# Masks behind both heads' products, inverse sums a step later, and a reordered turn to the routed mixture

## The chip, the cores and the metric

The kernel runs on one core of a Trainium2 chip. The metric is device time in microseconds (us), the median of several runs. The profile is one execution on the same kind of core. Its engines are called PE (TensorE matmuls), PEld (TensorE weight loads), DVE (VectorE), ACT (ScalarE), POOL (GpSimd) and SP (SyncE, which here only issues DMAs). Each engine takes its instructions in the order in which they were written, and stands when the next one has to wait.

## The reference, cut to what matters

Three layers follow one another on 1152 tokens of 512 numbers.

```python
# 1. attention, 2 batches x 8 heads, 576 positions, 64 wide, with a decay
scores = scale * q @ k.T
decay  = cum[:, None] - cum[None, :]              # cum: running sum of log f
scores = where(causal, -1e9, scores + decay)
attn   = exp(scores - max(scores)); attn /= attn.sum(-1) + 1e-9
x      = attn @ v
# 2. dense mixture, 4 experts of 512 -> 1024 -> 512, every token through all of them
out   += p[:, e] * (relu(x @ w1[e]) @ w2[e])
# 3. routed mixture, 8 experts: tokens with x @ w_skip <= 0 pass through,
#    the others go through the one expert with the largest logit
y[mask] = gate_w[mask] * (relu(xc[mask] @ w1[e]) @ w2[e]);  out = x + y
```

## The kernel before, in words

**Attention** (span 0 to about 115 us) goes over eight pairs of heads, numbered 0 to 7, and in each over five steps. Steps 0 to 3 take 128 queries each against 128, 256, 384 and 512 keys, head by head; step 4 takes the last 64 queries of both heads together. `emit_s` (line 238) writes a step's scores: for each head a product with the rounded keys (L247, tile kh), a product with what the rounding left over (L248, kl), and a bf16 product that adds the causal mask (L249); the three add into one PSUM tile. Then DVE adds the bias and finds the maximum (L252, tile sn), and ACT takes the exponential and its sum (L255, tile e). Step 4 does the same with L266 to L278 and the tile e_t. At the end of step 4, DVE adds 1e-9 to the sums of the whole pair (L281, rs) and inverts them (L282), and ACT spreads them into a tile rsx (L284).

`emit_tp` (line 287) follows two steps behind: PE transposes the exponentials (L298; for step 4 L309 and L313), ACT copies the first head's result out of PSUM (L301, tile et) and DVE the second head's (L303). With step 4 PE also transposes rsx (L321) and the inverse sums (L322). `emit_av` (line 332) follows three steps behind with the products with v. The loop at line 470 writes, for each step n, first `emit_tp` of step n-2, then `emit_s` of step n, then `emit_av` of step n-3, and then what prepares the next pair.

That preparation is `split_k` and `split_q` (lines 215 and 226): DVE rounds the next pair's keys (L224, kh) and queries (L229, qa), and POOL subtracts the rounded from the full values (two of L232 into kl, two of L235 into qa, 64 partitions each). For pair 1 they are written in step 2 of pair 0, for the others in step 0 of the pair ahead. From pair 4 on, steps 1 and 4 also split a quarter of a weight tile of the dense mixture: an ACT cast (L146) and a POOL subtraction (L150).

**The dense mixture** (about 115 to 525 us) runs up products (L660 to L662) and down products (L675 to L677) back to back on PE. Nothing of it is edited.

**The turn** (about 525 to 538 us) finds each token's expert for the last blocks of tokens. `select` (L766) collects the first expert's tokens on PE, `logits` (L557) and `prefix` (L585, L587) are small PE products, `choose`, `keep`, `mine` and `pick` small DVE steps, and `heat` (L731) writes matmuls whose result nothing reads. Meanwhile the weights of the routed mixture arrive: SP loads them in chunks of 1 MB (L136) into a ring of 18 places.

**The routed mixture** (about 533 us to the end) goes over eight small tiles (`Few`, one for each expert, up to 64 tokens) and two larger ones for the rest (`Many`). For a tile, POOL gathers its tokens (L503), PE turns them (`x_in`, L879, copied out of PSUM by ACT in L880), `up` (L886) multiplies with the first weights in two halves, `turn` (L893) transposes, and `down` (L901) multiplies with the second weights. `place`, `spread` and `lists` (L994 to L1022) find which tokens the larger tiles take. From the second tile on, POOL also fetches weights of the larger tiles (L861), by an index that is only known then.

Of the kernel before, what the change touches and what calls it, by code (L numbers as in the profile page):

```python
# [13 lines left out]
ALU = mybir.AluOpType  # L14
# [32 lines left out]
def kernel(  # L47
# [116 lines left out]
    with ExitStack() as at:  # L164
# [61 lines left out]
        def split_q(p):  # L226
            raw, qa, kh, kl = [state[p][x] for x in ("raw", "qa", "kh", "kl")]
            rk = raw[:, QW:QKW].rearrange("p (h c) -> p h c", h=2)
            V.tensor_copy(out=qa, in_=raw[:, 0:QW])  # L229
            for h in range(2):  # L230
                rows = slice(64 * h, 64 * h + 64)
                G.tensor_tensor(out=kl[rows, h], in0=rk[rows, h], in1=kh[rows, h].bitcast(F32), op=ALU.subtract)  # L232
            for h in range(2):
                rows, cols = slice(64 - 64 * h, 128 - 64 * h), slice(TOPAD * h, TOPAD * h + TOPAD)
                G.tensor_tensor(out=qa[rows, cols], in0=raw[rows, cols], in1=qa[rows, cols].bitcast(F32),  # L235
                                op=ALU.subtract)

        def emit_s(p, i):
            st = state[p]
            qa, kh, kl, bi = st["qa"], st["kh"], st["kl"], st["bi"]  # L240
            if i < 4:
                w = P * (i + 1)
                n = max(256, w)
                for h in range(2):
                    ps = ps_s.tile([P, 512], F32, tag="s", name=f"s_{p}_{i}_{h}")
                    q0 = TOPAD * h + i * P
                    T.matmul(out=ps[:, :n], lhsT=qa[:, q0:q0 + P], rhs=kh[:, h, :n], start=True, stop=False)  # L247
                    T.matmul(out=ps[:, :n], lhsT=qa[:, q0:q0 + P], rhs=kl[:, h, :n], start=False, stop=False)  # L248
                    T.matmul(out=ps[:, i * P:w], lhsT=identb, rhs=maskd, start=False, stop=True)  # L249
                    sneg = e_p.tile([P, S], F32, tag="sneg", name=f"sn_{p}_{i}_{h}")  # L250
                    mn = sm_p.tile([P, 1], F32, tag="mn", name=f"mn_{p}_{i}_{h}")
                    V.tensor_tensor_reduce(out=sneg[:, :w], in0=ps[:, :w], in1=bi[:, h, :w], scale=-0.125,  # L252
                                           scalar=3.0e38, op0=ALU.add, op1=ALU.min, accum_out=mn)
                    e = e_p.tile([P, S], F32, tag=f"e{h}", name=f"e_{p}_{i}_{h}")
                    A.activation(out=e[:, :w], in_=sneg[:, :w], func=AF.Exp, bias=mn, scale=-1.0,  # L255
                                 accum_out=st["sum"][:, 2 * i + h:2 * i + h + 1])
                    st["E"][i, h] = e
            else:
                sneg = e_p.tile([P, S], F32, tag="sneg", name=f"sn_{p}_t")
                mns = []  # L260
                for half in range(2):
                    c0 = half * 288
                    ps = ps_s.tile([P, 512], F32, tag="s", name=f"s_{p}_t_{half}")
                    for h in range(2):
                        q0 = TOPAD * h + 512
                        T.matmul(out=ps[:, :288], lhsT=qa[:, q0:q0 + P], rhs=kh[:, h, c0:c0 + 288], start=(h == 0),  # L266
                                 stop=False)
                        T.matmul(out=ps[:, :288], lhsT=qa[:, q0:q0 + P], rhs=kl[:, h, c0:c0 + 288], start=False,
                                 stop=(half == 0 and h == 1))
                    if half == 1:  # L270
                        T.matmul(out=ps[:, 224:288], lhsT=identb, rhs=maskt, start=False, stop=True)
                    mn = sm_p.tile([P, 1], F32, tag="mn", name=f"mn_{p}_t_{half}")
                    V.tensor_tensor_reduce(out=sneg[:, c0:c0 + 288], in0=ps[:, :288], in1=bi[:, 2, c0:c0 + 288],
                                           scale=-0.125, scalar=(3.0e38 if half == 0 else mns[0]),
                                           op0=ALU.add, op1=ALU.min, accum_out=mn)
                    mns.append(mn)
                e = e_p.tile([P, S], F32, tag="e0", name=f"e_{p}_t")
                A.activation(out=e, in_=sneg, func=AF.Exp, bias=mns[1], scale=-1.0,  # L278
                             accum_out=st["sum"][:, 8:9])
                st["E"][4] = e  # L280
                V.tensor_scalar(out=st["rs"], in0=st["sum"], scalar1=1e-9, scalar2=None, op0=ALU.add)  # L281
                V.reciprocal(out=st["sum"], in_=st["rs"])  # L282
                rsx = st["rs"] = sm_p.tile([P, 4, P], F32, tag="rsx", name=f"rsx_{p}", bufs=1)
                A.copy(out=rsx.rearrange("p j (h c) -> p (j h) c", h=2),  # L284
                       in_=st["sum"][:, 0:8].unsqueeze(2).to_broadcast([P, 8, 64]))

        def emit_tp(p, i):
            st = state[p]
# [181 lines left out]
        for n in range(2, len(steps) + LAG_AV):  # L470
            if 0 <= n - LAG_TP < len(steps):
                emit_tp(*steps[n - LAG_TP])
            if n < len(steps):
                p, i = steps[n]
                emit_s(p, i)
# [50 lines left out]
    with ExitStack() as mo:  # L526
# [237 lines left out]
        def select(t):  # L764
            for g in range(2):
                T.matmul(out=xsel[RT * g:RT * g + RT, 0:HD], lhsT=sel[:, t - NX, :],  # L766
                         rhs=acc[:, t, g * HD:(g + 1) * HD], start=(t == NX), stop=(t == L))
# [4 lines left out]
        choose(L - 1)  # L772
        mine(L - 1)
        count(L - 1)
        for t in range(NX, NA):
            select(t)
        logits(L, ps_u.tile([P, 512], F32, tag="u", name=f"lg_{L}"))
        keep(L - 1)
        prefix(L - 1, pf)
        heat(6)  # L780
        choose(L)
        pf = ps_u.tile([P, 512], F32, tag="u", name="pf_L")
        prefix(L, pf)
        mine(L)
        pick(L - 1)
        select(L - 1)
        pick(L)
        select(L)
# [20 lines left out]
    xes = [xs0] + [xe_p.tile([P, HD], F32, name=f"xe_{e}") for e in range(1, E2)]  # L809
    xos = [xe_p.tile([P, DM], F32, name=f"xo_{k}") for k in range(KO)]  # L810
    G.memset(xes[1], 0.0)
    for x in xes[2:]:
        A.copy(out=x, in_=zero.to_broadcast([P, HD]))
    xt_p = pool(ctx, "xt", 1, "right")
    wraw2 = pool(ctx, "wraw2", 4, "right")
    for k in range(14, RING):
# [199 lines left out]
        V.tensor_tensor(out=gt, in0=f[:, :, 4], in1=gt, op=ALU.add)  # L1016

    def lists():
        po = tpx[:, 0:KO * 5 * E2].rearrange("p (k j e) -> p k j e", k=KO, j=5)
        for t in range(NB):  # L1020
            for k in range(KO):
                T.matmul(out=po[:, k], lhsT=oho[:, t, k, :], rhs=perm[:, t, :, :], start=(t == 0 and k == 0),  # L1022
                         stop=(t == NB - 1 and k == KO - 1))
        listed(po, KO, idxo, gato)
# [4 lines left out]
    load_m(14, NS + 2)  # L1029
    tiles[0].up(0)  # L1030
    tiles[0].up(1)
    for x in xos:
        A.copy(out=x, in_=zero.to_broadcast([P, DM]))
    gates()
    tiles[0].turn()
    tiles[1].x_in()
    tiles[0].down()
    place()
    tiles[1].up(0)
    tiles[1].up(1)  # L1040
    spread(0, NB)
    tiles[2].x_in()
    ahead = {E2 - 3: (0, 0), E2 - 2: (1, 0), E2 - 1: (0, 1), E2: (1, 1)}
    behind = [i for i in range(len(chunks)) if chunks[i][1] >= E2]
    for i in range(1, len(tiles)):
# [115 lines left out]
```

## Time and profile before

| | |
|---|---|
| median of 3 runs | 633.64 us (633.6 to 636.07) |
| the profiled execution's own time | 633.03 us |
| its span | 631.3 us |
| mean granted TensorE clock | 0.991 |
| PE busy | 613.6 us (97%) |
| DVE busy | 251.1 us (40%) |
| ACT busy | 202.1 us (32%) |
| POOL busy | 177.6 us (28%) |

The profile's times are those of one execution, in us from the start of the span. A row of the timeline gives start, duration, engine, line, operation, output and inputs, shapes, and how many instructions of one kind were merged into it (x8). A bracket tells how long the engine had been idle before and what ended that. PE's ends are modelled: matmuls overlap, so what a matmul costs is the distance from its start to the next one's. PEclk is the granted clock as a share of 2.4 GHz: 1.00 is the upper of the two levels, 0.50 the lower (1.2 GHz).

### The profile page before, as it was taken

The page shows a single profiled execution, that of the slowest core. Times are in us where ns is not written, and L with a number is a line of the kernel's source. Part 1 is how long each engine was busy: PE and PEld are TensorE (multiplying, and loading weights), DVE is VectorE, ACT ScalarE, POOL GpSimd, SP SyncE. Part 2 cuts the span into 40 slices and gives each one's busy share as a digit, 9 for nine tenths or more (in the row PEclk, how much of TensorE's full clock was granted, in tenths as well). Part 3 has the DMA queues.
Part 4 walks back from the last instruction along what each step waited for, and adds up shares of the span by engine and source line. Part 5 has one row for each costly group of instructions (what it writes and reads, how often), then busy time and mean ns, then how long its engine had stood idle before and what let it go on. Part 6 is the DMA issues. An engine that isn't in the chain of part 4 may idle for free. (4 is left out here: it accounts for less than half of the span.)

```text
span 631.3 us, 9528 instructions
## 1 busy us (share of the span) xinstructions
PE 613.6 (97%) x3773; PEld 514.6 (82%) x3773; DVE 251.1 (40%) x686; ACT 202.1 (32%) x480; POOL 177.6 (28%) x160
## 2 busy tenths in 40 slices
PE   8899999999999999999999999999999999899995
PEld 5788777988899999999999999998888975455674
DVE  6777776222222222222222222222223577411753
ACT  5678887422122122122122122112202112211661
POOL 5755883223033033033023013102200000532411
PEclk7999999999999999999999999999999999999998
DMA  6768570211011021001201101205705457999930
GB/s 205 225 249 307 194 245 2 69 66 67 0 67 68 0 67 41 26 7 61 67 1 66 67 1 66 67 0 226 308 17 214 169 188 268 360 422 423 413 144 24
DMA packets 20415, 86.50 MB, mean 137 GB/s; under 512 B 3086, under 2 KB 4120, under 8 KB 13200
## 3 DMA queue, kind: packets, MB, share of 16 engines
q1 hardware_dynamic: 14816, 69.52, 29.8%
q0 software_dynamic: 2240, 10.32, 4.1%
q10 hardware_dynamic: 3312, 6.03, 2.6%
q8 instruction: 30, 0.49, 0.3%
q14 instruction: 17, 0.14, 0.1%
HBM read 79.44 MB, written 7.64 MB: 138 GB/s over the span
## 5 line engine op out<-in xcount | busy, mean ns | idle before, releaser
L150 POOL TENSOR_TENSOR wl<-raw,wh 128x512 fp32r<-128x512 f32 x64 | 82.8, 1294 | 272.4 <-ACT wh L146 272.4
L663 ACT ACTIVATE hh<-u 128x384 fp32r<-128x384 f32 x96 | 47.2, 491 | 298.9 <-PE u L662 294.9
L661 PE MATMUL u<-xtl,wh 128*128 128x384 f32 x384 | 129.4, 337 | 0.0
L662 PE MATMUL u<-xth,wl 128*128 128x384 f32 x384 | 129.2, 337 | 0.0
L660 PE MATMUL u<-xth,wh 128*128 128x384 f32 x384 | 129.2, 336 | 0.0
L675 PE MATMUL dn<-wh,hh 128*128 128x512 f32 x288 | 114.8, 399 | 0.0
L676 PE MATMUL dn<-wl,hh 128*128 128x512 f32 x288 | 113.8, 395 | 0.0
L677 PE MATMUL dn<-wh,hl 128*128 128x512 f32 x288 | 113.3, 393 | 0.0
L664 DVE SCALAR_TENSOR_TENSOR hl<-u,hh 128x384 fp32r<-128x384 f32 x96 | 53.5, 557 | 149.6 <-ACT hh L663 149.5
L687 DVE SCALAR_TENSOR_TENSOR acc<-dn,dps,acc 128x512 f32<-128x512 f32 (+1 forms) x64 | 47.4, 742 | 109.9 <-PE dn L677 109.9
L661 PEld LDWEIGHTS u<-xtl,wh 128*128 128x128 f32 x384 | 72.2, 188 | 1.0
L660 PEld LDWEIGHTS u<-xth,wh 128*128 128x128 f32 x384 | 72.2, 188 | 0.9
L662 PEld LDWEIGHTS u<-xth,wl 128*128 128x128 f32 x384 | 72.2, 188 | 0.0
L677 PEld LDWEIGHTS dn<-wh,hl 128*128 128x128 f32 x288 | 54.1, 188 | 12.3
L675 PEld LDWEIGHTS dn<-wh,hh 128*128 128x128 f32 x288 | 54.1, 188 | 10.8
L676 PEld LDWEIGHTS dn<-wl,hh 128*128 128x128 f32 x288 | 54.2, 188 | 10.2
L255 ACT ACTIVATE e<-sn,mn 128x128 f32<-128x128 f32 (+3 forms) x64 | 35.6, 557 | 14.8 <-DVE mn L252 14.6
L146 ACT CAST wh<-raw 128x512 fp32r<-128x512 f32 x64 | 39.2, 612 | 0.0
L252 DVE CUSTOM_DVE_ANT_0 sn<-s,bias 128x128 f32<-128x128 f32 (+3 forms) x64 | 29.3, 485 | 7.6 <-PE s L249 4.8
L886 PE MATMUL up<-wm,xt 128*64 128x512 f32 x128 | 30.3, 598 | 0.9 <-ACT xt L880 0.6
L901 PE MATMUL yp<-wm,ht 128*64 128x256 f32 x256 | 29.1, 380 | 0.0
L247 PE MATMUL s<-kh,qa 128*128 128x256 f32 (+2 forms) x64 | 27.1, 423 | 1.6 <-POOL qa L235 1.0
(228 smaller groups left out, 717.1 us busy)
## 6 DMA issues: line engine op xcount, KB each, us to landing
wm<-in_m SPq DMA_DIRECT2D x32, 1024.0 KB, 11.4
raw<-in_w SPq DMA_DIRECT2D x16, 1024.0 KB, 4.9
qk<-in_qk SPq DMA_DIRECT2D x7, 640.0 KB, 6.0
qk<-in_qk SPq DMA_DIRECT2D x7, 576.0 KB, 4.4
bias<-nbd SPq DMA_DIRECT2D x14, 288.0 KB, 6.0
v<-in_v SPq DMA_DIRECT2D x8, 320.0 KB, 3.0
bias<-nbd SPq DMA_DIRECT2D x16, 144.0 KB, 5.8
xd<-acc ACTq DMA_DIRECT2D x9, 256.0 KB, 2.1
```

The lines of the kernel that those rows point to most:

```text
L146: A.copy(out=o, in_=i) if eng is A else eng.tensor_copy(out=o, in_=i)
L150: eng.tensor_tensor(out=ws[k][1][:, c, :], in0=wr[k][:, c, :], in1=ws[k][0][:, c, :].bitcast(F32), op=ALU.subtract)
L255: A.activation(out=e[:, :w], in_=sneg[:, :w], func=AF.Exp, bias=mn, scale=-1.0, accum_out=st["sum"][:, 2 * i + h:2 * i + h + 1])
L660: T.matmul(out=ps[:, :TT], lhsT=wh[:, c, js], rhs=xth[:, c, ts], start=(c == 0), stop=False)
L661: T.matmul(out=ps[:, :TT], lhsT=wh[:, c, js], rhs=xtl[:, c, ts], start=False, stop=False)
L662: T.matmul(out=ps[:, :TT], lhsT=wl[:, c, js], rhs=xth[:, c, ts], start=False, stop=(c == KD - 1))
L663: A.activation(out=hh[:, j, :], in_=ps[:, :TT], func=AF.Relu)
L664: V.scalar_tensor_tensor(out=hl[:, j, :], in0=ps[:, :TT], scalar=0.0, in1=hh[:, j, :].bitcast(F32), op0=ALU.max, op1=ALU.subtract)
L675: T.matmul(out=ps, lhsT=hh[:, j, ks], rhs=wh[:, j, :], start=(j == 0), stop=False)
L676: T.matmul(out=ps, lhsT=hh[:, j, ks], rhs=wl[:, j, :], start=False, stop=False)
L677: T.matmul(out=ps, lhsT=hl[:, j, ks], rhs=wh[:, j, :], start=False, stop=(j == 3))
L687: V.scalar_tensor_tensor(out=a, in0=ps[:, c0:c1], scalar=pe, in1=a, op0=ALU.mult, op1=ALU.add)
```

## The change

- In `emit_s`, steps 0 to 3, both heads' products (two each) are written first, then both masks, then both heads' DVE and ACT work.
- The three instructions that invert a pair's sums leave the end of step 4 and become `emit_inv`, written one step later, behind the transposes of step 3 and ahead of the next pair's first scores.
- For pair 1, the second of the two query subtractions (L235) goes from POOL to DVE.
- In the turn, one block is selected ahead of the last block's logits and the other behind `prefix`; `heat(6)` becomes `heat(2)`; `mine` and `pick` of the last blocks go ahead of the last `prefix`.
- The zero fill of two tiles (xo) goes ahead of the first up product; the third tile's `x_in` goes ahead of the second tile's second half; `lists` gets a PSUM tile of its own in place of the one that `x_in` uses.

```diff
--- before.py
+++ after.py
@@ -232,7 +232,7 @@
                 G.tensor_tensor(out=kl[rows, h], in0=rk[rows, h], in1=kh[rows, h].bitcast(F32), op=ALU.subtract)
             for h in range(2):
                 rows, cols = slice(64 - 64 * h, 128 - 64 * h), slice(TOPAD * h, TOPAD * h + TOPAD)
-                G.tensor_tensor(out=qa[rows, cols], in0=raw[rows, cols], in1=qa[rows, cols].bitcast(F32),
+                (V if p == 1 and h else G).tensor_tensor(out=qa[rows, cols], in0=raw[rows, cols], in1=qa[rows, cols].bitcast(F32),
                                 op=ALU.subtract)
 
         def emit_s(p, i):
@@ -241,12 +241,16 @@
             if i < 4:
                 w = P * (i + 1)
                 n = max(256, w)
+                pss = []
                 for h in range(2):
                     ps = ps_s.tile([P, 512], F32, tag="s", name=f"s_{p}_{i}_{h}")
                     q0 = TOPAD * h + i * P
                     T.matmul(out=ps[:, :n], lhsT=qa[:, q0:q0 + P], rhs=kh[:, h, :n], start=True, stop=False)
                     T.matmul(out=ps[:, :n], lhsT=qa[:, q0:q0 + P], rhs=kl[:, h, :n], start=False, stop=False)
+                    pss.append(ps)
+                for ps in pss:
                     T.matmul(out=ps[:, i * P:w], lhsT=identb, rhs=maskd, start=False, stop=True)
+                for h, ps in enumerate(pss):
                     sneg = e_p.tile([P, S], F32, tag="sneg", name=f"sn_{p}_{i}_{h}")
                     mn = sm_p.tile([P, 1], F32, tag="mn", name=f"mn_{p}_{i}_{h}")
                     V.tensor_tensor_reduce(out=sneg[:, :w], in0=ps[:, :w], in1=bi[:, h, :w], scale=-0.125,
@@ -278,11 +282,14 @@
                 A.activation(out=e, in_=sneg, func=AF.Exp, bias=mns[1], scale=-1.0,
                              accum_out=st["sum"][:, 8:9])
                 st["E"][4] = e
-                V.tensor_scalar(out=st["rs"], in0=st["sum"], scalar1=1e-9, scalar2=None, op0=ALU.add)
-                V.reciprocal(out=st["sum"], in_=st["rs"])
-                rsx = st["rs"] = sm_p.tile([P, 4, P], F32, tag="rsx", name=f"rsx_{p}", bufs=1)
-                A.copy(out=rsx.rearrange("p j (h c) -> p (j h) c", h=2),
-                       in_=st["sum"][:, 0:8].unsqueeze(2).to_broadcast([P, 8, 64]))
+
+        def emit_inv(p):
+            st = state[p]
+            V.tensor_scalar(out=st["rs"], in0=st["sum"], scalar1=1e-9, scalar2=None, op0=ALU.add)
+            V.reciprocal(out=st["sum"], in_=st["rs"])
+            rsx = st["rs"] = sm_p.tile([P, 4, P], F32, tag="rsx", name=f"rsx_{p}", bufs=1)
+            A.copy(out=rsx.rearrange("p j (h c) -> p (j h) c", h=2),
+                   in_=st["sum"][:, 0:8].unsqueeze(2).to_broadcast([P, 8, 64]))
 
         def emit_tp(p, i):
             st = state[p]
@@ -470,6 +477,8 @@
         for n in range(2, len(steps) + LAG_AV):
             if 0 <= n - LAG_TP < len(steps):
                 emit_tp(*steps[n - LAG_TP])
+                if steps[n - LAG_TP][1] == 3:
+                    emit_inv(steps[n - LAG_TP][0])
             if n < len(steps):
                 p, i = steps[n]
                 emit_s(p, i)
@@ -772,17 +781,18 @@
         choose(L - 1)
         mine(L - 1)
         count(L - 1)
-        for t in range(NX, NA):
-            select(t)
+        select(NX)
         logits(L, ps_u.tile([P, 512], F32, tag="u", name=f"lg_{L}"))
         keep(L - 1)
         prefix(L - 1, pf)
-        heat(6)
+        for t in range(NX + 1, NA):
+            select(t)
+        heat(2)
         choose(L)
+        mine(L)
+        pick(L - 1)
         pf = ps_u.tile([P, 512], F32, tag="u", name="pf_L")
         prefix(L, pf)
-        mine(L)
-        pick(L - 1)
         select(L - 1)
         pick(L)
         select(L)
@@ -809,8 +819,8 @@
     xes = [xs0] + [xe_p.tile([P, HD], F32, name=f"xe_{e}") for e in range(1, E2)]
     xos = [xe_p.tile([P, DM], F32, name=f"xo_{k}") for k in range(KO)]
     G.memset(xes[1], 0.0)
-    for x in xes[2:]:
-        A.copy(out=x, in_=zero.to_broadcast([P, HD]))
+    for x in xes[2:] + xos:
+        A.copy(out=x, in_=zero.to_broadcast([P, x.shape[1]]))
     xt_p = pool(ctx, "xt", 1, "right")
     wraw2 = pool(ctx, "wraw2", 4, "right")
     for k in range(14, RING):
@@ -1016,7 +1026,7 @@
         V.tensor_tensor(out=gt, in0=f[:, :, 4], in1=gt, op=ALU.add)
 
     def lists():
-        po = tpx[:, 0:KO * 5 * E2].rearrange("p (k j e) -> p k j e", k=KO, j=5)
+        po = ups[3][:, 0:KO * 5 * E2].rearrange("p (k j e) -> p k j e", k=KO, j=5)
         for t in range(NB):
             for k in range(KO):
                 T.matmul(out=po[:, k], lhsT=oho[:, t, k, :], rhs=perm[:, t, :, :], start=(t == 0 and k == 0),
@@ -1029,17 +1039,15 @@
     load_m(14, NS + 2)
     tiles[0].up(0)
     tiles[0].up(1)
-    for x in xos:
-        A.copy(out=x, in_=zero.to_broadcast([P, DM]))
     gates()
     tiles[0].turn()
     tiles[1].x_in()
     tiles[0].down()
     place()
     tiles[1].up(0)
+    tiles[2].x_in()
     tiles[1].up(1)
     spread(0, NB)
-    tiles[2].x_in()
     ahead = {E2 - 3: (0, 0), E2 - 2: (1, 0), E2 - 1: (0, 1), E2: (1, 1)}
     behind = [i for i in range(len(chunks)) if chunks[i][1] >= E2]
     for i in range(1, len(tiles)):
```

## Rows read from the trace of the kernel before

**Rows 1.** Timeline of PE, 42.0 to 49.3: pair 2 and the next pair's start.
```profile
42.17 0.48 PE L247 MATMUL s<-kh,qa 128*128 128x512 f32 x1
42.49 0.40 PE L248 MATMUL s<-kl,qa 128*128 128x512 f32 x1
42.73 0.23 PE L249 MATMUL s<-maskd,identb 128*128 128x128 bf16 x1
42.76 0.48 PE L247 MATMUL s<-kh,qa 128*128 128x512 f32 x1
...
46.04 1.09 PE L298 MATMUL tp<-ident,e 128*128 128x128 f32 x8
...
48.81 0.60 PE L321 MATMUL rp<-ident,rsx 128*128 128x128 f32 x4
```

**Rows 2.** Waits, 20 to 127: who waited for whom, us in total, times, longest.
```profile
PE tp_t L309 <- DVE et L303: 2.6, 6, 1.1
```

**Rows 3.** Timeline of DVE, 43.0 to 48.4, the same stretch.
```profile
43.10 0.69 DVE L252 CUSTOM_DVE_ANT_0 sn<-s,bias 128x512 f32<-128x512 f32 x1 [0.23 <-ACT xth L354]
...
47.01 0.17 DVE L281 TENSOR_SCALAR rs<-sum 128x9 f32<-128x9 f32 x1 [1.00 <-ACT e_t L278]
...
47.34 0.63 DVE L303 COPY et<-tp 128x512 f32<-128x512 f32 x1
47.89 0.28 DVE L252 CUSTOM_DVE_ANT_0 sn<-s,bias 128x128 f32<-128x128 f32 x1
```

**Rows 4.** Timeline of ACT, 43.8 to 49 (pair 2) and 70.4 to 73.9 (pair 4).
```profile
46.10 0.78 ACT L278 ACTIVATE e_t<-sn_t,mn_t 128x576 f32<-128x576 f32 x1 [0.38 <-DVE mn_t L273]
...
47.52 0.62 ACT L284 COPY rsx<-sum 128x512 f32<-128x512 f32 x1 [0.55 <-DVE sum L282]
48.04 0.58 ACT L301 COPY et<-tp 128x512 f32<-128x512 f32 x1
...
72.43 0.62 ACT L146 CAST wh<-raw 128x512 fp32r<-128x512 f32 x1
```

**Rows 5.** Timelines of DVE, POOL and PE in the first pair, 6 to 24.5.
```profile
6.20 1.29 DVE L414 TENSOR_TENSOR qa<-qk,qa 64x256 fp32r<-64x256 f32 x2
...
11.89 1.14 DVE L414 TENSOR_TENSOR qa<-qk,qa 64x384 fp32r<-64x384 f32 x2
...
16.87 3.42 POOL L232 TENSOR_TENSOR kl<-qk,kh 64x576 fp32r<-64x576 f32 x2 [1.33 <-DVE kh L224]
20.25 3.16 POOL L235 TENSOR_TENSOR qa<-qk,qa 64x640 fp32r<-64x640 f32 x2
...
21.59 0.24 DVE L281 TENSOR_SCALAR rs<-sum 128x9 f32<-128x9 f32 x1 [1.00 <-ACT e_t L278]
...
23.46 0.39 PE L247 MATMUL s<-kh,qa 128*128 128x256 f32 x1 [1.04 <-POOL qa L235]
...
24.43 0.27 PE L321 MATMUL rp<-ident,rsx 128*128 128x128 f32 x1
```

**Rows 6.** Timeline of PE in the turn and the routed mixture, 526.3 to 592.
```profile
530.36 1.08 PE L766 MATMUL xsel<-acc,sel 128*64 128x256 f32 x8 [0.55 <-DVE sel L761]
...
538.28 0.44 PE L879 MATMUL tpx<-ident,xe 128*128 128x128 f32 x2 [0.23 <-DMA xe<-xd,idx]
...
546.75 1.94 PE L886 MATMUL up<-wm,xt 128*64 128x512 f32 x8 [0.61 <-ACT xt L880]
...
550.12 0.44 PE L879 MATMUL tpx<-ident,xe 128*128 128x128 f32 x2 [0.40 <-DVE found L1013]
...
591.68 0.60 PE L901 MATMUL yp<-wm,ht 128*64 128x256 f32 x4
```

**Rows 7.** DMA issues, 560.65 to 561: size, us from issue to landing.
```profile
wm<-in_m SPq DMA_DIRECT2D x1, 1024.0 KB, 30.5
```

**Rows 8.** Busy time of each engine by stretch (then PEclk, DMA share, GB/s).
```profile
9.30:16.00 6.70, 6.70 (x23) 4.52 (x23) 4.35 (x13) 3.58 (x13) 5.63 (x18) 0.50 0.56 181
560.00:580.00 20.00, 20.00 (x146) 10.57 (x144) 2.30 (x5) 3.08 (x7) 6.08 (x6) 1.00 1.01 422
```

## The prediction, made before the change was run

> **What bounds the kernel now.** I read the busy times first: PE 613.6 of 631.3 us, so an edit is worth what it takes out of PE's stream or puts into it. Then the waits: in the attention PE stands at the transposes of step 4, in all 2.6 us and six times [rows 2], and in the first pair 1.04 on POOL's queries [rows 5]. Then the timelines around these places [rows 1, 3 to 5], the turn and the routed mixture [rows 6], and last the DMA view: from about 545 us on the weight stream is the limit, with a DMA share of 1.01 and 422 GB/s [rows 8]. The granted clock is at its upper level there; in the first pair, from 9.3 to 16.0, it is at the lower one, 0.50 [rows 8].
>
> **Masks behind both heads.** In step 3 of pair 2 the first head's products start at 42.17 and 42.49, its mask at 42.73, the second head's at 42.76 [rows 1]: 0.32, 0.24 and 0.03 start to start. The product that follows a mask costs 0.32, the one that follows a product 0.24, so I read 0.08 as the change from a mask to a product. The old step is 0.32 + 0.24 + 0.03 + 0.32 + 0.24 = 1.15 to the second mask. The new one is 0.32 + 0.24 + 0.24 + 0.24 + x, where x is the first mask with a mask behind it. No row shows that: its bounds are 0.03, as with a product behind it, and 0.23, a mask's own length [rows 1]; I take 0.03, since that row too has the next instruction on its heels. So 1.07 in place of 1.15: 0.08 saved a step, with x at its upper bound 0.12 lost. The Trainium skill ("TensorE: Matmul & The Clock Gate", section "Step-by-step: what each phase is for") says that weight loads are pulled ahead of matmuls that are still running; by that rule nothing is exposed that could be saved, and the time would be that of the third rival, 634.6. The 0.32 against 0.24 speaks against it here.
>
> Over a pair that is 4 x 0.08 = 0.32, but in pairs 1 to 6 the wait at step 4 takes it back, unless the wait moves too. What the grouping delays is the first head: its mask comes behind three more products, some 0.46 later in its step, 0.30 after the 0.16 gained in two steps before. So DVE's sn [rows 3] goes from 43.10 to 43.40, e_t [rows 4] from 46.10 to 46.40, and its sum is ready for rs at 47.31 in place of 47.01.
>
> **Inverse sums a step later.** Before, rs [rows 3] stood at the head of DVE's queue and waited 1.00 for e_t's sum, with the copy L303 (47.34) behind it; on ACT the copy rsx waited 0.55 for the inverse, with L301 (48.04) behind it [rows 4]. The transposes L309 wait for L303's buffer [rows 2]. New: the eight transposes of step 3 [rows 1] start at 46.04 - 0.24 (three grouped steps) = 45.80 and end, by the row's length of 1.09, at 46.89. L303 then starts at 46.94 in place of 47.34, with nothing ahead of it, and rs 0.55 behind it (as 47.89 - 47.34 [rows 3]), at 47.49, later than 47.31, so e_t's sum does not decide. From rs to rsx 0.51 (47.01 to 47.52), its copy 0.62 [rows 4]: 48.00 and 48.62. The transposes L321 need rsx and start 0.07 later, 48.69 in place of 48.81 [rows 1]. So the wait at L309 goes, and what is late next is rsx at L321: the gain is 0.12 a pair in pairs 1 to 3, 0.36.
>
> In pairs 4 to 6 a cast of weights, L146 of 0.62 [rows 4], stands in ACT's queue too. Before it was behind rsx; now it goes ahead, into the time in which ACT waits. L146 from 47.31 (e_t done), L301 from 47.83, rsx from 48.35, L321 at 49.04. Before, the cast shifted all this by 0.52, to 48.81 + 0.52 = 49.33. So 0.29 a pair, 0.87. In pair 7 the products of the dense mixture fill PE and nothing waits at step 4: three masks' gain, 0.24, stays. Cost of the edit below and above: at worst the whole 0.40 by which L303 is earlier is lost to a rsx that is 0.4 later, at best all 2.6 of [rows 2] goes.
>
> **Pair 1's second query on DVE.** It is one of two instructions that POOL does in 3.16 [rows 5]. What it costs DVE: L414 is the same operation, 1.14 for two of 384 columns, so 0.57 x 640/384 = 0.95. But DVE and POOL hinder one another: two L414 of 256 columns took 1.29 beside POOL [rows 5], where 0.57 x 256/384 = 0.38 each, 0.76 together, was due; and POOL's two L232 took 3.42 for 576 columns, where 3.16 x 576/640 = 2.84 was due, 0.58 more. I read this as one standing until the other's instruction is done. POOL does the first half (3.16 / 2 = 1.58, less what it has before DVE arrives) while DVE is to begin the second; that half then begins late by up to a POOL instruction of 1.42 to 1.58 and lasts 0.95. I take 1.42 + 0.95 = 2.37 on DVE's chain, and 0.2 for masks that come later in the first pair. rs was at 21.59 [rows 5]: now 24.16; with 0.51, 0.62 and 0.07 as above L321 is at 25.36 in place of 24.43, **+0.9**. PE's waits of 1.04 (at 23.46, for POOL's qa [rows 5]) and of 0.46 behind it go, but the later one hides that. Bounds: all of the 1.04 + 0.46 gained, -1.5; DVE also standing behind the second L232 (1.4 more), +2.3. Without standing, DVE is only 0.95 later, L321 comes by 23.9, -0.5.
>
> **The turn.** `heat` is shorter by four, `mine` and `pick` stand ahead of `prefix`, and the 0.55 for which L766 waited on sel [rows 6] can go: 0.5 to 0.75 on PE. Behind it, the first `x_in` (538.28) waits for the gather of its tokens and PE stands 0.23 on it [rows 6]; the gather follows a chain of DMAs that PE's products of this stretch do not hold up. I cost this at 0; it can gain 0.55 if the chain moves along, and lose as much if the gather is later.
>
> **The routed mixture.** The zero fill on ACT is at another place and beside PE: 0. The third tile's `x_in` ahead removes the 0.61 for which L886 stood on xt at 546.75, and the PSUM tile for `lists` the 0.40 at 550.12 on found [rows 6], together 1.01. But this stretch then meets the stream: the eight-tile's `down` of expert 6 starts at 591.68 [rows 6], and its weights, issued at 560.65 to 561 with 30.5 to land [rows 7], land at about 591.2. The issue does follow PE's release of a place, but the DMA engines are full [rows 8], so an earlier issue lands no sooner. PE can come 0.46 earlier there, no more; POOL's fetches, which begin 1 us sooner and share the same 422 GB/s, should put the stream's chunk later by some 0.3: **-0.15**. Bounds: all 1.01 gained, or 0.54 lost (a chunk 1 us later, 0.46 of it covered).
>
> **The sum** against the profiled execution, 633.03 (its span 631.3 and 1.7 around it): +0.9 - 0.36 - 0.87 - 0.24 - 0.15 = -0.72, 632.3. The median is 633.64, 0.61 above that execution, so on its scale **632.9**.
>
> **The rivals.** All on the median's scale.
> - *DVE does not stand behind POOL in pair 1.* The first pair gives -0.5 in place of +0.9: 631.5. For it: POOL's first half may be over before DVE comes; against it, both pairs of rows on L414 and L232. Chance 0.20.
> - *The stream is earlier too*, all of 1.01 is gained: 632.9 - 0.86, near 632.0. Against it the full DMA. 0.08.
> - *The mask grouping does not do what it says*: a weight load is no dearer behind a mask, and the 0.08 comes from elsewhere. Then the transposes of step 3 start at 46.04, L303 at 47.18, rs at 47.73 and L321 at 48.93, 0.12 later than before in pairs 1 to 3; in pairs 4 to 6 at 49.28, 0.05 earlier than 49.33; pair 7 gains nothing. Sum: 0.9 + 0.36 - 0.15 - 0.15 = +0.96, 634.6. Against it, both products behind a mask [rows 1] show the 0.32. 0.10. The Trainium skill's rule above would have it so.
> - *All bubbles go*: -2.6 [rows 2], -1.04 [rows 5] and 0.08 in each of 32 steps, in all -6.2: 627.4. Against it, rsx is on the chain. 0.08.
> - *Slower: the softmax of step 4 becomes the bound.* The place is e_t's sum. I have it at 47.31, and rs can take it at 47.49: 0.18 to spare. If grouping delays the first head's sn by more, since DVE and ACT take one head after the other and the copies L303 and L301 are now among them, every us beyond 0.18 goes to rs, rsx and L321. At 1.0 us late (one more copy of 0.58 to 0.63 [rows 3, 4] ahead of it on each of DVE and ACT, less what fits between) L321 is 0.82 later than worked out: 49.51 against 48.81 in pairs 1 to 3, 49.86 against 49.33 in 4 to 6. That is 3 x 0.70 + 3 x 0.53 = +3.7 where the forecast has -1.2: 637.8. 0.08.
> - *Less heat, and the clock falls in the turn.* At the lower level, seen over 6.7 us in the first pair [rows 8], such a stretch costs half its length, 3.3: 636.2. Against it: PE has real products on both sides. 0.04.
>
> **How the numbers follow.** The forecast has 0.42, with a range of its own from 631.6 to 634.2 (first pair within +-0.8, tail within +-0.5). The range of 8 in 10 leaves out the case of all bubbles and the slower one on step 4 (0.16) and takes in the others, the fall of the clock too: 630.2 to 636.3. About 0.5%, 3.2 us, is what a measurement of this kernel can tell from no change. Faster by more, under 630.5: the case of all bubbles, 0.08, and the ends of the first two rivals, 0.06: 0.14. Slower by more, above 636.8: the step-4 case and a tail of the clock's: 0.09. Within: 0.77.
>
> **What would show it.** In the timeline of PE, the step's products all some 0.24 apart but the first, and the first mask 0.05 ahead of the second. In the waits, no L309 on L303, and L321 on ACT's rsx instead, 0.1 to 0.3 before 48.9 in pair 2. In the first pair, L414's neighbour on DVE, the new subtraction, lasting well over 0.95 or starting late, rs near 24.2 and L321 near 25.3. In the tail, L886 and L879 without their waits, and a wait on wm at the `down` of expert 6. I am wrong if e_t's sum comes later than 47.5 in pair 2, if wm is not waited for there, or if PEclk shows 0.50 between 526 and 540.

## The result, and the profile after

The changed kernel takes 639.35 us (median of 6 executions, 638.67 to 640.08) against 633.91 (6 executions): ratio 1.0083, 95% interval 1.0069 to 1.0097. It is slower by 5.4 us where 0.7 faster was forecast, and outside the range of 630.2 to 636.3.

The profiled execution spans 637.7 us, 6.4 more than before. The start of the transposes of rsx (L321, now L328) marks the end of a pair's sums. These starts cut the difference up; each row is a start in one profiled execution, read from the timelines of PE:

| stretch | before | after | difference |
|---|---|---|---|
| start to rsx of pair 0 | 24.43 | 27.72 | +3.29 |
| pairs 1 to 3, from rsx to rsx | 12.19, 12.19, 12.20 | 12.44, 12.45, 12.45 | +0.75 |
| pairs 4 to 6 | 12.70, 12.71, 12.86 | 13.55, 13.54, 13.55 | +2.35 |
| pair 7 | 12.72 | 13.55 | +0.83 |
| last rsx to the last dense down product | 412.58 | 413.09 | +0.5 |
| from there to the first `x_in` | 13.70 | 13.57 | -0.13 |
| first `x_in` to the end | 93.04 | 91.86 | -1.18 |

So the attention lost 7.2, and the routed mixture gave back 1.2. The 0.5 behind the attention belongs to it too: in the timelines of PE, ten of the dense mixture's up products run ahead of L321 of pair 7 before, and only seven ahead of L328 after. Three products of 0.17 start to start have moved behind that cut, which makes 0.52, and without this pair 7 would have lost 1.35 and not 0.83.

The waits of PE, 20 to 127 us, after; columns as in [rows 2] (line, waited for whom, us in total, times, longest):

```profile
PE rp L328 <- ACT rsx L291: 6.6, 8, 1.3
PE tp L305 <- DVE et L310: 2.0, 1, 2.0
PE tp_t L316 <- DVE et L310: 0.8, 3, 0.3
PE tp_t L316 <- DVE rs L288: 0.3, 1, 0.3
```

The 2.6 us of [rows 2] are 0.8 and 0.3 now, but PE waits 6.6 for rsx, in all eight pairs: the wait has moved from the copy of the transposed scores to the copy of the inverse sums. What makes rsx late differs from pair to pair.

**Pairs 4 to 7.** Timeline of DVE, ACT and POOL in pair 6, after:

```profile
102.60 0.18 ACT L282 ACTIVATION_READ_ACCUMULATOR e_t<-sn_t,mn_t 128x1 f32 x1
102.69 0.60 ACT L146 CAST wh<-raw 128x512 fp32r<-128x512 f32 x1
102.78 0.69 DVE L310 COPY et<-tp 128x512 f32<-128x512 f32 x1 [0.17 <-PE tp L305]
103.20 0.57 ACT L308 COPY et<-tp 128x512 f32<-128x512 f32 x1
103.37 1.27 POOL L150 TENSOR_TENSOR wl<-raw,wh 128x512 fp32r<-128x512 f32 x1 [1.64 <-ACT wh L146]
103.39 1.27 DVE L288 TENSOR_SCALAR rs<-sum 128x9 f32<-128x9 f32 x1
...
104.70 0.21 DVE L289 RECIPROCAL sum<-rs 128x9 f32<-128x9 f32 x1
...
105.00 0.62 ACT L291 COPY rsx<-sum 128x512 f32<-128x512 f32 x1 [1.23 <-DVE sum L289]
...
105.67 0.66 PE L328 MATMUL rp<-ident,rsx 128*128 128x128 f32 x4 [1.31 <-ACT rsx L291]
```

An addition to nine numbers in each partition (rs, 0.17 in [rows 3]) lasts 1.27, exactly as long as POOL's subtraction L150, which started 0.02 earlier: DVE stands until POOL is done. Before, ACT's cast L146 came behind rsx [rows 4], and POOL's subtraction, which waits for that cast, started after the inverse. Now the cast is free as soon as e_t is done (102.69), and POOL starts just as DVE comes to rs.

**Pairs 1 to 3.** Timelines of PE, DVE and ACT in pair 2 after, beside [rows 1], [rows 3] and [rows 4]:

```profile
45.61 0.49 PE L248 MATMUL s<-kh,qa 128*128 128x512 f32 x1
...
45.94 0.40 PE L249 MATMUL s<-kl,qa 128*128 128x512 f32 x1
...
46.18 0.40 PE L248 MATMUL s<-kh,qa 128*128 128x512 f32 x1
...
46.41 0.40 PE L249 MATMUL s<-kl,qa 128*128 128x512 f32 x1
46.65 0.28 PE L252 MATMUL s<-maskd,identb 128*128 128x128 bf16 x2
46.77 1.07 PE L305 MATMUL tp<-ident,e 128*128 128x128 f32 x6
46.88 0.36 ACT L308 COPY et<-tp 128x256 f32<-128x256 f32 x1
47.02 0.69 DVE L256 CUSTOM_DVE_ANT_0 sn<-s,bias 128x512 f32<-128x512 f32 x1 [0.43 <-ACT xth L361]
...
49.69 1.09 PE L305 MATMUL tp<-ident,e 128*128 128x128 f32 x8
...
50.82 0.69 DVE L310 COPY et<-tp 128x512 f32<-128x512 f32 x1 [0.97 <-PE tp L305]
...
51.43 0.16 DVE L288 TENSOR_SCALAR rs<-sum 128x9 f32<-128x9 f32 x1
...
51.93 0.62 ACT L291 COPY rsx<-sum 128x512 f32<-128x512 f32 x1 [0.64 <-DVE sum L289]
...
52.60 0.66 PE L328 MATMUL rp<-ident,rsx 128*128 128x128 f32 x4 [0.50 <-ACT rsx L291]
```

The products now start 0.33, 0.24, 0.23 and 0.24 after one another, and the step lasts 1.16 (45.61 to 46.77). The old one ran from 42.17 [rows 1] to the transposes of the next line, from the timeline of PE before, 1.21: some 0.06 saved.

```profile
43.38 0.82 PE L298 MATMUL tp<-ident,e 128*128 128x128 f32 x6
```

The six transposes behind the new step last longer, though (1.07 for 0.82), for they wait for the tile that ACT's copy (46.88) has still to empty; the waits of the weight loads show it, 40 to 127 us, after:

```profile
PEld tp L305 <- ACT et L308: 2.6, 12, 0.3
```

From the transposes at 49.69 to L328 it takes 2.91; before, 46.04 to 48.81, 2.77 [rows 1].

**The first pair.** Timeline of DVE, POOL and PE after, beside [rows 5]:

```profile
17.07 0.75 DVE L224 CAST kh<-qk 128x1152 fp32r<-128x1152 f32 x1
...
17.91 3.86 POOL L232 TENSOR_TENSOR kl<-qk,kh 64x576 fp32r<-64x576 f32 x2 [2.04 <-DVE kh L224]
...
18.59 1.90 DVE L235 TENSOR_TENSOR qa<-qk,qa 64x640 fp32r<-64x640 f32 x1
20.41 0.41 DVE L310 COPY et<-tp 128x256 f32<-128x256 f32 x1
20.75 0.67 DVE L256 CUSTOM_DVE_ANT_0 sn<-s,bias 128x512 f32<-128x512 f32 x1
20.88 0.65 PE L305 MATMUL tp<-ident,e 128*128 128x128 f32 x3 [2.00 <-DVE et L310]
```

The stretch from 22 to 23 us after, in the columns of [rows 8] (PEclk is the third from the end):

```profile
22.00:23.00 1.00, 1.00 (x6) 1.00 (x5) 0.89 (x4) 1.00 (x5) 1.00 (x1) 0.50 1.01 224
```

DVE's query subtraction lasts 1.90, twice its estimate of 0.95, beside POOL's L232. PE stands 2.00 for the copy queued behind it, and after that stand its granted clock is at the lower level, 0.50.

The lower level is not new in this pair: before, it held from 9.3 to 16.0 [rows 8]. What differs ahead of 16 us is how long the same products take. The bias products of 16x128, from the timelines of PE before and after:

```profile
5.91 0.71 PE L420 MATMUL b<-cum,neg 16*128 16x128 f32 x4
5.91 1.22 PE L427 MATMUL b<-cum,neg 16*128 16x128 f32 x4
```

The next ones take 0.70 at 8.52 before and 1.22 at 8.89 after. That points to the lower level, but PEclk reads 1.00 in this stretch after, so the cause is not shown.

**The turn and the routed mixture.** Waits of PE, 525 to 640 us, after:

```profile
PE tpx L889 <- DMA xe<-xd,idx: 0.9, 1, 0.9
PE tp L903 <- ACT hs L899: 0.4, 1, 0.4
PE up L896 <- ACT ex L627: 0.3, 1, 0.3
PE yp L977 <- ACT hth L968: 0.2, 1, 0.2
PE xsel L775 <- DVE sel L770: 0.2, 1, 0.2
```

The 0.61 on xt and the 0.40 on found of [rows 6] are gone; 0.23 on the gather has become 0.9, which is where the turn's gain ended.

### The profile page after: what moved, and what is told of

Read it like the earlier page. It is cut to its first block, busy times and chain, and to the rows that moved or that the text cites. A ratio compares the mean times of both kernels' runs of the same rounds, so it can differ in the third digit from the quotient of the medians.

```text
span 637.7 us, 9522 instructions
## 1 busy us (share of the span) xinstructions
PE 616.6 (97%) x3769; PEld 517.2 (81%) x3769; DVE 255.7 (40%) x687; ACT 201.9 (32%) x480; POOL 175.8 (28%) x159
## 5 line engine op out<-in xcount | busy, mean ns | idle before, releaser
L150 POOL TENSOR_TENSOR wl<-raw,wh 128x512 fp32r<-128x512 f32 x64 | 82.5, 1289 | 271.8 <-ACT wh L146 271.8
L146 ACT CAST wh<-raw 128x512 fp32r<-128x512 f32 x64 | 39.1, 611 | 0.0
L232 POOL TENSOR_TENSOR kl<-qk,kh 64x576 fp32r<-64x576 f32 x14 | 23.5, 1680 | 24.0 <-DVE kh L224 15.3
```

The source lines that it names most:

```text
L146: A.copy(out=o, in_=i) if eng is A else eng.tensor_copy(out=o, in_=i)
L150: eng.tensor_tensor(out=ws[k][1][:, c, :], in0=wr[k][:, c, :], in1=ws[k][0][:, c, :].bitcast(F32), op=ALU.subtract)
```

## The experiments

The theory from this profile: in pairs 4 to 7 DVE's small inverse stands for POOL's subtraction; the masks and the inverse each lengthen the chain that ends in L328; the first pair pays for DVE's query. The chief rival: the pairs are long because the softmax is late in all of them, and rs beside L150 is a coincidence. Medians are against runs of the kernel before on the same chip (633.7 to 633.9).

**1. The inverse back at the end of step 4.**

```diff
                 st["E"][4] = e
+                emit_inv(p)
...
-                if steps[n - LAG_TP][1] == 3:
-                    emit_inv(steps[n - LAG_TP][0])
```

> The changed kernel with the inverse of the sums back at the end of step 4. Theory: in pairs 4 to 7 the first instruction of the inverse lasts 1.25 to 1.27 us in place of 0.17, because POOL's weight subtraction starts at the same moment; with the inverse early it lasts 0.17 again, each of these pairs takes about 12.8 in place of 13.5, and the time is 636 to 637. Rival, that these pairs are longer for the masks behind both heads (a chain that is late everywhere): 639 to 640, pairs of 13.5 as now.

635.79 us, ratio 1.0031 (1.0016 to 1.0046). rs lasts 0.17 to 0.18 in all pairs, and pairs 4 to 7 take 12.96, 12.95, 13.11 and 12.96 in place of 13.5. That is the theory's side (the time is 0.2 under its range). But 0.25 of the excess of 0.84 remains, and pairs 1 to 3 stay at 12.44: the masks cost something by themselves.

**2. The cast and the subtraction behind the inverse.** Step 4's `split_h` and `split_l` are written one step later, behind `emit_inv`:

```diff
                 if steps[n - LAG_TP][1] == 3:
                     emit_inv(steps[n - LAG_TP][0])
+                    weights(steps[n - LAG_TP][0], 4)
...
-                if p >= 4 and i in (1, 4):
+                if i == 1:
+                    weights(p, 1)
```

> The changed kernel with step 4's weight cast and POOL's subtraction written behind the inverse, one step later, so that POOL's instruction can no longer start beside it. Theory: the first instruction of the inverse lasts 0.17 in pairs 4 to 7, they take 12.4 to 12.6 in place of 13.5, and the time is 635 to 636. Rival, that ACT and not DVE is the bound there: the 0.6 of the cast is only moved, pairs of 13.2 to 13.5, 638 to 639.5.

635.94 us, ratio 1.0025 (1.0013 to 1.0036). The timeline of DVE in pairs 4 to 6:

```profile
76.05 0.16 DVE L288 TENSOR_SCALAR rs<-sum 128x9 f32<-128x9 f32 x1
...
88.49 0.16 DVE L288 TENSOR_SCALAR rs<-sum 128x9 f32<-128x9 f32 x1
...
101.52 0.16 DVE L288 TENSOR_SCALAR rs<-sum 128x9 f32<-128x9 f32 x1
```

Pairs 4, 5 and 7 take 12.45, 12.44 and 12.48, as long as pairs 1 to 3 (pair 7 with seven dense products in it, as after the change); pair 6 takes 13.03. With the cast out of the way nothing is left of the loss that only these pairs had, save in pair 6, and there the same standing is at another place. DVE has the four instructions of `shares` ahead of the copy L310 in that pair, and one of them meets a subtraction of POOL; timelines of DVE and POOL:

```profile
99.49 1.03 DVE L470 TENSOR_SCALAR dsum<-dsum 128x9 f32<-128x9 f32 x1
99.08 1.41 POOL L362 TENSOR_TENSOR xtl<-xo,xth 128x576 fp32r<-128x576 f32 x1
```

In the changed kernel the same L470 takes 0.17 (at 101.96). Here it ends 0.03 after POOL.

**3. POOL's subtraction in two halves.** The dose: the same work of POOL, in pieces of half the length.

```diff
-                    split_l(k, G, c)
+                    if i == 4:
+                        for a in (0, 256):
+                            G.tensor_tensor(out=ws[k][1][:, c, a:a + 256], ...)
```

> The changed kernel with POOL's weight subtraction of step 4 in pairs 4 to 7 written as two instructions of 256 columns. Theory: DVE's first instruction of the inverse stands until the POOL instruction at work ends, so it lasts about half of 1.27, 0.6 to 0.8, and these pairs take 12.9 to 13.1. Rival, that DVE only runs slower for as long as POOL works at all, or is late for another cause: it lasts 1.2 to 1.3 as before, pairs of 13.5.

635.97 us, ratio 1.0040 (1.0025 to 1.0056). The timeline of DVE in pairs 4 and 5:

```profile
74.78 0.71 DVE L288 TENSOR_SCALAR rs<-sum 128x9 f32<-128x9 f32 x1
...
87.78 0.71 DVE L288 TENSOR_SCALAR rs<-sum 128x9 f32<-128x9 f32 x1
```

The timeline of POOL there (two instructions in a row):

```profile
74.74 1.41 POOL L511 TENSOR_TENSOR wl<-raw,wh 128x256 fp32r<-128x256 f32 x2 [1.65 <-ACT wh L146]
...
87.74 1.41 POOL L511 TENSOR_TENSOR wl<-raw,wh 128x256 fp32r<-128x256 f32 x2 [1.62 <-ACT wh L146]
```

POOL is busy for 1.41, longer than before, and rs lasts 0.71, half of that: it stands until the instruction at work ends, not for as long as POOL works. The pairs follow: 12.45 with rs at 0.16, 13.00 at 0.71 and 13.55 at 1.27, one us of pair for one us of rs. Of all runs this tells most. The four pairs are worth 2.2 of the 3.4 us between this time and the changed kernel's; in the profiled executions the first pair is shorter too (see below).

**4. The inverse alone on the kernel before.**

> Only the inverse one step later, masks and all else as before. Theory: rsx comes 0.15 to 0.2 later after the transposes than before, so pairs 1 to 3 take 12.35 to 12.40 in place of 12.19; in pairs 4 to 7 POOL's subtraction starts with the inverse, whose first instruction lasts 1.1 to 1.3, and they take 13.3: 636.2 to 637.2. Rival, the forecast's step (the inverse behind the copy is no later than before): 12.1 to 12.2 and 12.4, 632.5 to 633.

637.17 us, ratio 1.0053 (1.0038 to 1.0067). Pairs 1 to 3 take 12.39 to 12.40, pairs 4 to 7 13.31 with rs at 1.07 to 1.09. The forecast's step fails by itself: 2.91 from the eight transposes to those of rsx here too (59.54 to 62.45 in pair 3).

**5. The masks alone on the kernel before.**

> Only the masks behind both heads' products, all else as before. Theory: the grouping saves PE 0.06 to 0.08 in a step and makes DVE and ACT late by 0.3 to 0.35, which comes back as a wait of the transposes of step 2 for ACT's copy (0.25) and of the transposes of step 4: pairs 1 to 3 take 12.44 in place of 12.19, pairs 4 to 7 12.96 in place of 12.70 to 12.86, the first pair 1.1 to 1.8 more: 636.2 to 637.2. Rival, the forecast's step: 0.08 a step saved, pairs no longer than 12.19, and only the first pair later: 633.5 to 634.8.

637.13 us, ratio 1.0055 (1.0040 to 1.0069). Pairs 2 and 3 take 12.43, pairs 4 to 7 12.95 to 13.11; pair 1 takes 13.38, with PEclk at 0.50 in 24 to 26 us. In step 3 the masks' order saves 0.06, and the transposes behind it stand 0.25 for ACT's copy, which comes behind two exponentials and a cast (xth) that all start later as the first head's scores do; at the end of the pair PE stands 4.3 us in six places from 20 us on where it stood 2.6 in six [rows 2], 3.7 in five of them from 40 us on. Its waits, 40 to 127 us:

```profile
PE tp_t L317 <- DVE et L311: 3.7, 5, 1.4
```

**6. Each mask behind its own head, all else as changed.**

```diff
                     pss.append(ps)
-                for ps in pss:
```

> The changed kernel with each mask directly behind its own head's products again. Theory: the first pair gains back some 1.1 us (its first maximum at 7.9 in place of 9.0); in pairs 1 to 3 the wait of the transposes of step 2 for ACT's copy (0.25 a pair) goes, while 0.06 to 0.08 is lost in each of three steps, so a pair stays at 12.38 to 12.45; pairs 4 to 7 keep the standing inverse: 638.0 to 638.4. Rival, that the grouping is what lengthens all pairs: pairs 1 to 3 at 12.2, pairs 4 to 7 at 12.7, 634.5 to 635.5.

637.36 us, ratio 1.0064 (1.0049 to 1.0078), 0.6 under the theory's range. Pairs 1 to 3 take 12.40, pairs 4 to 7 13.31 to 13.32. Taking the masks away alone gives back little in a pair, as taking the inverse away alone did: either edit is enough to bring pairs 1 to 3 from 12.19 to 12.4, and both together make 12.44. That is one reason why the parts (3.4 and 3.3 us by experiments 4 and 5) don't add up to the whole.

**7. Pair 1's second query back on POOL.**

```diff
-                (V if p == 1 and h else G).tensor_tensor(out=qa...
+                G.tensor_tensor(out=qa...
```

> The changed kernel with pair 1's second query subtraction back on POOL. Theory: on DVE that instruction lasted 1.90 us, half of it standing beside POOL's subtraction of the keys, and it stands ahead of step 2's copy and step 3's maxima in the first pair (sn of step 3 at 20.75 in place of 17.77); back on POOL, sn of step 3 starts at about 18.8, the first transposes of rsx at 25.8 to 26.3 in place of 27.72, less a wait for POOL's qa of up to 1.0: 637.4 to 638.4. Rival, that the first pair is late for the masks and the inverse alone and PE then waits for POOL's queries for as long as it had waited for DVE: 639.4, unchanged.

638.61 us, ratio 1.0064 (1.0052 to 1.0077), 0.2 above the theory's range: 0.7 less than the changed kernel by the medians; the intervals of the two ratios overlap. From L224 to sn of step 3 DVE takes 1.74, and 3.68 in the changed kernel: 1.94 for that instruction. But the rs of the first pair then meets POOL's query subtraction and stands itself. DVE in the first pair of this run:

```profile
23.06 1.39 DVE L288 TENSOR_SCALAR rs<-sum 128x9 f32<-128x9 f32 x1
```

Pair 1 takes 13.15 in this execution, but not for that: in the profile of experiment 11 rs stands for 1.39 too and pair 1 takes 12.20. What the long ones (13.38 in experiment 5, 13.11 in experiment 9) share is the lower clock: PEclk is 0.50 in 25 to 27 us here and in experiment 9.

**8. The tail alone** (the attention as before).

> The turn and the routed mixture as changed, the whole attention as before. Theory: the two waits of PE in the routed mixture (0.6 on xt, 0.4 to 0.56 on found) go and the weight stream, which follows PE's releases, comes earlier too; the turn gives next to nothing, as the first x_in waits for its gather: 632.4 to 632.9. Rival, the forecast's step: the weights of expert 6 land when they landed before, and PE waits for them there for all but 0.15: 633.5.

632.97 us, ratio 0.9987 (0.9975 to 0.9999), 0.1 above the theory's range. In its profiled execution PE stood 1.84 us for the gather, and behind that its clock was down; the stretch from 539 to 544 us, columns as in [rows 8]:

```profile
539.00:544.00 5.00, 5.00 (x33) 2.96 (x34) 0.00 (x0) 0.37 (x1) 3.78 (x5) 0.66 0.94 385
```

That is the rival of the lower clock in the turn, for this execution; it is not in the changed kernel's own profile, where the clock is at the upper level through the turn and the routed mixture up to 635 us. Of the eight profiled executions with two warming products one more has it: in experiment 1 PEclk is 0.57 in 532 to 536, inside the turn, and eight L774 products take 1.97 where L766 took 1.08 [rows 6]. None of the six with six warming products has it.

**9. The tail with six warming products.**

```diff
-        heat(2)
+        heat(6)
```

> Turn and routed mixture as changed but with six warming products in place of two; attention as before. Theory: with two, PE stood 1.8 us for the gather in the profiled execution of this tail and its clock fell behind it (0.66 in 539 to 544), which is why the time without the attention edits spread from 631.3 to 635.2; with six the stand is shorter by about 0.85, the clock stays at 1.00 and the time is 631.8 to 632.6. Rival: the gather's landing alone decides, and the spread and the median stay (632.9 to 633.3).

633.37 us, ratio 0.9991 (0.9977 to 1.0004), spread 631.2 to 634.8. The theory missed: neither median nor spread improves, though the clock holds through the turn in the profiled execution. The spread is not made by the clock in the turn alone.

**10. Only the edits behind the turn.**

> Only the edits behind the turn (zero fill, third x_in, lists in a PSUM tile of its own); turn and attention as before. Theory: PE's waits of 0.6 and 0.4 to 0.56 go, some 0.2 comes back as a wait for the weights of expert 6: 632.6 to 633.0, and from the first x_in to the down product of expert 6 some 52.3 in place of 53.4. Rival: the stream lands as before, 633.4 to 633.8.

633.10 us, ratio 0.9997 (0.9985 to 1.0008). From the first `x_in` to the down product of expert 6 it took 52.13 (539.34 to 591.47), before 53.40: the 1.0 and more is there, and the down product takes 3.55 as before, so nothing of it is lost to the weights in this execution. The median is 0.6 below the kernel before and 0.1 above the theory's range; the executions spread over 3 us, and the interval doesn't tell it from no change.

**11 and 12. Experiment 10 and experiment 8, each with step 4's cast one step later** but the inverse early: `weights(steps[n - LAG_TP][0], 4)` behind `emit_tp` of step 3.

> Routed mixture as changed, turn and attention as before, but in pairs 4 to 7 the cast and the subtraction of step 4 are written one step later, behind the copies of the next transposes (and behind rsx, which stays early). Theory: the cast no longer delays ACT's copy, and POOL's subtraction meets no instruction of the inverse: pairs 4 to 7 take 12.2 to 12.3 in place of 12.70 to 12.86, 630.6 to 631.4. Rival: POOL's subtraction now meets DVE's maxima or the rounding of the next queries and they stand, pairs of 12.7 to 13.2, 632.8 or more.

632.41 us, ratio 0.9974 (0.9961 to 0.9987), 1.0 above the theory's range. Pair 4 takes 12.20, and no wait of the cast is left there; the 12.19 of pair 7 has three dense products fewer in it (0.52), which come behind. Pairs 5 and 6 take 12.58 and 12.87: their rs lasts 0.57 and 0.39, so the subtractions meet it in part.

> The same with the changed turn as well (two warming products). Theory: as the run with the old turn less 0 to 0.5 where the clock holds, more by up to 2 where it falls: median 630.5 to 632, with a wider spread. Rival, that the turn's edits gain their whole 0.7: 629.9 to 630.5, no wider.

632.40 us, ratio 0.9984 (0.9973 to 0.9995), 0.4 above the theory's range; pairs 4 to 7 at 12.20, 12.41, 12.90 and 12.19. By the medians both are 1.3 us faster than the kernel before and don't differ from one another; some 0.6 of it is that of experiment 10.

## Why the prediction was wrong

**The step that failed**: "Before it was behind rsx; now it goes ahead, into the time in which ACT waits." For ACT that was right as far as rsx shows it: the cast takes 0.60 at 102.69, and rsx at 105.00 had waited 1.23 for DVE. But the cast releases POOL's subtraction, and the prediction never asked what that would meet: of the moved instruction it counted the engine's queue and not what it triggers on another engine. The standing costs 1.10 (1.27 - 0.17) in each of four pairs, 4.4 us. Without it pairs 4 to 6 would take 12.45 (experiment 2, pairs 4 and 5), 0.25 less than before, where the prediction had 0.29 less; with it they take 13.55. Experiments 2 and 3 show it. That 0.25 is near 0.29 is in part luck: experiment 2 takes the cast out of ACT's queue as well, and the forecast had the start of the transposes wrong (see the inverse). The prediction had even read the same standing in the first pair [rows 5] and priced it there, but looked for it only where an instruction was moved between these two engines. The Trainium skill (page "SBUF — State Buffer", section "Who interferes with whom") has the rule: of DVE's instructions, a `tensor_scalar` can take a port pair that POOL needs too, and whoever is second stands for the whole instruction of the first. The 0.71 beside halves and 1.27 beside wholes agree.

**The masks.** 0.24 saved over three steps: 0.20 was measured (0.06, 0.08, 0.06), so a product behind a mask does cost more than one behind a product; that its weight load is the cause was not tried. The delay of the first head was foreseen (sn 0.30 later) and followed to e_t only; there it came as forecast (from L321 or L328 of pair 1 to the end of e_t's sum 10.35 before, 10.66 after), and rs did not wait for it. It came back earlier, at the transposes of step 2, which wait 0.25 for a tile that ACT has to empty: the rival on the softmax had the right mechanism and the wrong place. That the pairs end later, at 12.43, is shown by experiment 5; that it is ACT's copy is read from its waits and was not tried by itself.

**The inverse.** From the transposes to L321, 2.89 were worked out (45.80 to 48.69) and 2.91 measured. What failed is the start: the transposes came not 0.24 earlier but 0.12 later after the previous L321 (9.54 for 9.42), by the masks above and by 0.05 for the transposes of rsx, which take 0.49 to the next start behind their wait (40.15 to 40.64) and took 0.44 before. So +0.25 a pair, not -0.12. Without the masks (experiment 4) it is still +0.20: the inverse early had 2.77 there.

**The first pair**: +0.9 forecast, +3.3 in the profiled executions. The 2.37 for DVE's query measured 1.94 or 1.95 (experiments 6 and 7), so the standing was read rightly; not foreseen was that PE stands 2.00 for it and that its clock then falls. What the fall costs, experiment 3 shows, whose first pair is written as in the changed kernel. There PE stood 1.72, its clock stayed at 1.00 in 21 to 24, and from the transposes behind the stand (20.87) to L328 it took 5.30; the changed kernel took 6.84 (20.88 to 27.72): 1.54. Another 1.03 is there before L224, and most of it goes with the execution and not with the edit. In the nine profiled executions in which the first bias products take 1.22, L224 starts at 16.84 to 17.07; in the five in which they take 0.71 to 0.97, at 15.48 to 16.35; both kinds occur with the masks as before and behind both heads. Like against like, experiment 3 against experiment 10 (the attention as before, bias products of 1.22, no fall), the transposes of rsx come at 26.17 for 25.26: +0.91, as forecast, in one execution of each. With 0.83 by which experiment 10 is later than the kernel before (25.26 for 24.43) and the 1.54 this makes 3.28 of the 3.29. In the six profiled executions whose first two pairs are written as in the kernel before (its own and experiments 8 to 12), pair 1 ends at 36.08 to 39.04. Which of these first pairs the executions behind the medians had is not on record, so how much of the 5.4 us is the first pair's stays open: 0.9 like against like, and up to 2.4 more by what differs from execution to execution.

**The turn** at 0 was right (-0.13), by the gather, as worked out. **The routed mixture**: -0.15 was mis-sized, -1.18 measured. The landing was rightly taken as almost fixed: from the first `x_in` 52.96 passed before and 52.68 after, 0.28 less where 0.3 more was costed. What was read wrongly is the slack. PE's weight loads for expert 6 after:

```profile
597.59 0.14 PEld L911 LDWEIGHTS yp<-wm,ht 128*64 128x64 f32 x2 [0.29 <-DVE ht L904]
598.01 0.14 PEld L911 LDWEIGHTS yp<-wm,ht 128*64 128x64 f32 x2 [0.29 <-issue]
598.60 2.79 PEld L911 LDWEIGHTS yp<-wm,ht 128*64 128x64 f32 x28 [0.45 <-DMA wm<-in_m]
```

The chunk is needed from the fifth of 32 loads on, not from the first, so PE could come earlier still than by the 0.46 that were read off the first product, by some 0.4 (four of 32 products that took 3.55). It came 1.27 earlier (52.13 for 53.40), and the down product took 3.76 for 3.55. The rival of an earlier stream came true in its time, and only 0.28 of its mechanism did.

**After the attention** 0.5 more passes up to the last dense product, in every run that writes the inverse or the cast later (413.0 to 413.2) and in none of the others (412.5 to 412.7). In all of the first, seven dense up products run ahead of the transposes of rsx in pair 7, in all of the others ten. So this is work that changed sides, not a loss of its own.

**The signs of being wrong** that the prediction named did not come: e_t's sum was not late, the chunk for expert 6 was waited for (0.45), and PEclk did not fall in the turn. None of them was about POOL beside rs.

## What to carry to other kernels

When an instruction is moved, follow what it releases on other engines, and look for DVE instructions that will then run beside a POOL instruction: here even nine elements a partition waited until it ended. A wait on PE can be worth keeping if the chain behind it is only just shorter; where two chains end within 0.1 to 0.2 us of one another, a later head is paid for by both. When a landing bounds a product, look which of its loads first needs the chunk: here it was the fifth.

## What the runs showed of the hardware

A DVE addition of 128x9 numbers took 0.16 to 0.18 alone, 0.71 beside POOL instructions of half of 1.41, 1.27 beside one of 1.27 and 1.39 beside a query subtraction of half of 3.15 on POOL; another of 128x9 (L470) took 1.03 beside POOL's L362 and 0.17 alone. PE's granted clock was at the lower level after stands of 2.00 us (first pair, 0.50 in 22 to 23) and 1.84 us (experiment 8, 0.66 over 539 to 544), and at 1.00 after the stand of 0.87 in the changed kernel and after one of 1.72 (experiment 3, 21 to 24). In experiment 1 it was at the lower level in 532 to 536 with PE busy all through (4.00 of 4.00).
